# Gated linear attention with two feed-forward layers on one Trainium2 core: heads' data stored in rows 16 to 111 without gaps

## The chip, the cores and the metric

The kernel runs on one core of one Trainium2 chip. The metric is the device time of one execution in microseconds (us), lower is better. Before the change the median of 3 runs is 915.93 us (915.37 to 917.22). The profile shown here is one further execution. TensorE is called PE here, VectorE DVE, ScalarE ACT, GpSimd POOL; SP is the engine whose queue issues every DMA of this kernel.

## The reference

Three layers, one after the other. The first is a recurrence over 768 time steps for 4 batches and 8 heads of 48 dimensions; the other two are feed-forward layers of 384 to 2048 to 384 with an elementwise function between.

```python
def _attn_ref(q, k, v, alpha):                       # each (4, 8, 768, 48)
    state = np.zeros((B, H, D, D), dtype=np.float32)
    for t in range(S):
        state = alpha[:, :, t, :, None] * state + np.einsum('bhd,bhe->bhde', k[:, :, t], v[:, :, t])
        y[:, :, t] = np.einsum('bhd,bhde->bhe', q[:, :, t], state)
    return y
def _moe_ref(x, w_in, w_out, a, b):                  # x is (3072, 384), d_ff is 2048
    h = x @ w_in
    g = (a[0] + a[1]*h + a[2]*h**2 + a[3]*h**3) / (1 + abs(b[0])*abs(h) + abs(b[1])*h**2 + 1e-06)
    return g @ w_out
def _moe2_ref(x, w_in, w_out):
    h = x @ w_in
    return (h * np.cos(h)) @ w_out
```

## The kernel before

**Attention.** The sequence is cut into 6 chunks of 128 steps, and with 4 batches this makes 24 units (`NU`). A unit holds all 8 heads of one batch in one chunk: four pairs of heads (`HP`) lie side by side in the free dimension, and the two heads of a pair lie one above the other in the partitions (called rows here). A head has 48 dimensions, and its slot has 64 rows: head 0 uses rows 0 to 47, head 1 rows 64 to 111, and rows 48 to 63 and 112 to 127 hold padding (0 for keys and queries, 1 for the decay). The arrays `kqT`, `aT` and the output array `x0d` have this padding in DRAM too, so that each transfer takes 128 rows.

Per unit, `decay` makes the running product p of the decay (DVE, a scan), `guess` and `inverse0`, `inverse1` make its reciprocal (ACT, then DVE), `scale_q` and `scale_k` multiply queries by p and keys by the reciprocal (POOL, lines 310 and 305), `scores` makes the products of keys and queries (PE, L319), `mask0` and `mask1` copy and mask them (ACT, then POOL L333), `y_state` and `y_scores` make the outputs (PE, L386 and L396), `y_out` copies them from PSUM (ACT, L410) and `y_store` writes them to DRAM (L426). `transposes` (L341), `k_out` (L346), `update0` (L353) and `update1` carry the state into the next chunk.

**What sets the order.** `attention(n)` is called for slots n from -3 to 24; in slot n each stage works on its own unit: `decay` on n+3, `scale_q` and `scale_k` on n+1, `scores` on n, the outputs on n-1. The program order of each engine is the order of these calls. The loads are issued ahead, from SP, in the loop of lines 1288 to 1321:

```python
            if n >= 2:
                y_store(n - 2)
            ...
            if n >= -1:
                load(n + 5, "a")
            if n >= 0:
                load(n + 3, "kq")
                for i in range(SOME[n] if n <= LEAD else 0):
                    w_fetch(2 * NF)
                load(n + 2, "v")
```

Keys and queries (`kq`) have five buffers, the decay three, the copied outputs two (`kept[2:4]`). SP works in order, and the build gives every DMA of SP one of eight semaphores in turn; a DMA waits for the one eight places before it. Beside attention, the slots fetch the feed-forward weights (64-bit floats, `w_fetch`), which are cut into two parts by ACT, DVE and POOL (`tick`, `w_hi`, `w_lo` L212; two slots of three have one such weight tile), and from slot 8 on one `x_pieces` transfer a slot reads outputs back as the feed-forward input.

**Feed-forward layers.** From slot 20 (`LEAD`) on, `layers(n)` runs the first layer's steps, at first beside the last slots of attention, then alone; `threes(k)` runs most of the second with a scheme that needs fewer block products. These parts work on tiles of 128 rows in all dimensions, and `x_load` (lines 659 to 683) reads the attention's output array in pieces that leave out its padding rows.

**Before slot -3** the buffers' constant parts are set: `warm_up(13)` multiplies `ident` by itself, after POOL has set `ones`, the tails of `v_t`, `ident` and the tails of `s_all` (lines 1274 to 1286).

Of the kernel before, what the change touches and what calls it, by code (L numbers as in the profile page):

```python
# [24 lines left out]
NU = NC * B  # L25
H1 = 11
# [15 lines left out]
def attn_then_two_moe(ctx, tc, kqT, aT, vP, w1i, w1o, ma, mb, w2i, w2o, out):  # L42
# [5 lines left out]
    xd = [dram.tile([NC, B, 128 * HP, C], F32, name="x0d"), dram.tile([NC, DM, TB], F32, name="x1d")]  # L48
    x0d = dram.tile([2, B, 128 * HP, C], F32, name="x0")
# [64 lines left out]
    v_t = [const.tile([128, H * D + 64 - D], F32, tag=f"v{i}", name=f"v{i}") for i in range(4)]  # L114
# [3 lines left out]
    s_all = [const.tile([128, HP * D + 64 - D], F32, tag=f"s{b}", name=f"s{b}") for b in range(B)]  # L118
    s_c = [s[:, :HP * D].rearrange("p (a b) -> p a b", a=HP) for s in s_all]
# [110 lines left out]
    def load(u, name):  # L230


        if u >= NU:
            return
        c, b = divmod(u, B)
        ts = {"a": a_t, "kq": kq_t, "v": v_t}[name]
        t, src = ts[u % len(ts)], {"a": aT, "kq": kqT, "v": vP}[name][c, b]
        if name == "v":
            nc.sync.dma_start(out=t[:, :H * D], in_=src)
        elif u == 0 and name == "a":  # L240
            for cs in (slice(0, HP + HP // 2 * C), slice(HP + HP // 2 * C, HP * (C + 1))):
                nc.sync.dma_start(out=t[:, cs], in_=src[:, cs])
        else:
            nc.sync.dma_start(out=t, in_=src)
        d = U.setdefault(u, {})
        if name == "kq":
            d["k"], d["q"] = t[:, 0], t[:, 1]
        else:
            d[name] = t
# [5 lines left out]
    def sums(i, u, hs):  # L255
        at = NU if hs.start else u
        return chk[:, i, at:at + 1]


    def decay(u):  # L260
        d = U[u]
        d["p"] = in_p.tile([128, HP, C], F32, tag="p", name="p")
        a = d.pop("a")
        first, rest = a[:, :HP].unsqueeze(2), a[:, HP:].rearrange("p (a b) -> p a b", a=HP)
        for hs in parts(u):
            nc.vector.tensor_tensor(out=fresh[:, hs, 0:1], in0=first[:, hs], in1=fresh[:, hs, 1:2], op=ALU.max)
            nc.vector.tensor_tensor_scan(
                d["p"][:, hs].rearrange("p a b -> p (a b)"), rest[:, hs].rearrange("p a b -> p (a b)"),
                fresh[:, hs].rearrange("p a b -> p (a b)"), 0.0, ALU.mult, ALU.max,
            )  # L270

    def last_decay(u):
        d = U[u]
        d["pc"] = in_p.tile([128, HP, 1], F32, tag="pc", name="pc", bufs=6)
        nc.vector.tensor_tensor(out=d["pc"], in0=d["p"][:, :, C - 1:], in1=fresh[:, :, 1:2], op=ALU.max)


    def guess(u):
        d = U[u]
        d["r"] = bank("b1" if u == 1 else "r0", (128, HP, C))  # L280
# [6 lines left out]
    def inverse0(u, hs):  # L287
        d = U[u]
        if hs.start == 0:
            d["m"] = temp("ah", shape=(128, HP, C))  # L290
        nc.vector.scalar_tensor_tensor(
            d["m"][:, hs], d["p"][:, hs], RANGE, d["r"][:, hs], ALU.min, ALU.mult, accum_out=sums(1, u, hs)
        )

    def inverse1(u, hs):
        d = U[u]
        if hs.start == 0:
            d["n"] = temp("z", shape=(128, HP, C))
# [38 lines left out]
    def transposes(u):  # L337
        d = U[u]
        d["tp"] = bank("b0", (128, HP, 128))
        for hp in range(HP):  # L340
            nc.tensor.transpose(d["tp"][:, hp, :], d["k"][:, hp, :], ident)  # L341

    def k_out(u):
        d = U[u]
        d["kt"] = kept[u % 2]
        nc.scalar.activation(out=d["kt"], in_=d.pop("tp"), func=AF.Copy)  # L346

    def update0(u):
        d = U[u]
        d["u"] = ps_acc.tile([128, HP, D], F32, tag="acc2", name="u")  # L350
        for h in range(H):
            hp, j = divmod(h, 2)
            nc.tensor.matmul(  # L353
                d["u"][64 * j:64 * j + 64, hp, :], d["kt"][:, hp, 64 * j:64 * j + 64],
                d["v"][:, h * D:(h + 1) * D], start=True, stop=True,
            )

    def update1(u, tick):
        c, b = divmod(u, B)
        d = U[u]  # L360
        pc = d["pc"].to_broadcast([128, HP, D])
# [9 lines left out]
    def y_state(u):  # L371
# [48 lines left out]
    def y_store(u, rest=False):  # L420
# [5 lines left out]
        nc.sync.dma_start(out=to.rearrange("(p a) t -> p (a t)", a=HP), in_=t)  # L426
# [232 lines left out]
    def x_load(m, blk, kk):  # L659
# [7 lines left out]
        else:  # L667
            gap = (64 - D) * HP
            for p, row in {0: [(slice(0, 128), 0)], 1: [(slice(0, 64), 128), (slice(64, 128), 192 + gap)],
                           2: [(slice(0, 128), 256 + gap)]}[kk]:  # L670
                to_from = [(x, xd[0][blk])] if blk else [
                    (xt[0, 0][:, i, kk, :].bitcast(F32), x0d[i]) for i in range(2)
                ]
                for to, of in to_from:
                    rows = of[:, row:row + p.stop - p.start, :]
                    pieces.append(partial(
                        nc.sync.dma_start,
                        out=to[p].rearrange("p (b t) -> p b t", b=B), in_=rows.rearrange("b p t -> p b t")
                    ))
# [518 lines left out]
    def all_ok0():  # L1198
        nc.vector.tensor_tensor(out=chk[:, :, 0], in0=chk[:, :, 0], in1=chk[:, :, NU], op=ALU.add)
        nc.vector.tensor_scalar(ok[:, 0, :], chk[:, 0, :NU], -RANGE, None, ALU.is_ge)  # L1200
        nc.vector.tensor_scalar(ok[:, 1, :], chk[:, 1, :NU], -float(HP * C), None, ALU.add)
        nc.vector.tensor_tensor(out=ok[:, 1, :], in0=ok[:, 1, :], in1=ok[:, 1, :], op=ALU.mult)
        nc.vector.tensor_scalar(ok[:, 1, :], ok[:, 1, :], 0.0625, None, ALU.is_le)

    def all_ok1():
        cnt = bank("r1", (1, 2 * NU))
        nc.tensor.matmul(cnt, ones, ok.rearrange("p a b -> p (a b)"), start=True, stop=True)
        tot = const.tile([1, 1], F32, name="tot")
        nc.vector.tensor_reduce(tot, cnt, mybir.AxisListType.X, ALU.add)
        nc.vector.tensor_scalar(bad, tot, 128.0 * 2 * NU - 0.5, None, ALU.is_lt)  # L1210
# [52 lines left out]

    def warm_up(n):
# [5 lines left out]
    with tc.manual_schedule():  # L1270
# [13 lines left out]
        for s in s_all:  # L1284
            nc.gpsimd.memset(s[:, HP * D:], 0.0)
        warm_up(13)
        x_pieces = [p for kk in range(NK) for p in x_load(0, 0, kk)]
        for n in range(-3, NU + 1):
# [26 lines left out]
            if n == -3:  # L1315
                for name, u in (("v", 0), ("kq", 2)):
# [14 lines left out]
    def general():  # L1331
# [10 lines left out]
        for j in range(2):  # L1342
            nc.vector.memset(half[64 * j:64 * j + D, j:j + 1], 1.0)
        with tc.For_i(0, NC, 1) as c:
# [3 lines left out]
            q = fb.tile([128, B, HP, C], F32, name="q")  # L1348
            for b in range(B):
                nc.sync.dma_start(out=a[:, b], in_=aT[one, b].rearrange("o p t -> (o p) t"))  # L1350
                for i, t in enumerate((k, q)):
                    nc.sync.dma_start(out=t[:, b], in_=kqT[one, b, :, i].rearrange("o p a t -> (o p) a t"))
# [158 lines left out]
```

## Time and profile before

| | |
|---|---|
| median of 3 runs | 915.93 us (915.37 to 917.22) |
| the profiled execution's own time | 915.87 us |
| its span in the trace | 914.0 us |
| mean granted clock of PE | 0.997 of full speed |
| PE busy | 893.4 us (98% of the span) |
| DVE, ACT, POOL busy | 694.4, 697.1, 702.8 us |
| moved by DMA | 128.87 MB |

The span is the time from the first to the last recorded work; what lies around it is 1.87 us in this execution. Busy shares are means over the whole span, and the kernel has stages with different limits: attention takes about the first 105 us, and the rest is feed-forward work. So a change in attention is read in that stretch alone. A row of waits names the engine, the line that waited and what ended the wait last; a row of the chain gives start, length and what the end of the program hung on in that time.

### The profile page before, as it was taken

The page shows a single profiled execution, that of the slowest core. Times are in us where ns is not written, and L with a number is a line of the kernel's source. Part 1 is how long each engine was busy: PE and PEld are TensorE (multiplying, and loading weights), DVE is VectorE, ACT ScalarE, POOL GpSimd, SP SyncE. Part 2 cuts the span into 40 slices and gives each one's busy share as a digit, 9 for nine tenths or more (in the row PEclk, how much of TensorE's full clock was granted, in tenths as well). Part 3 has the DMA queues.
Part 4 walks back from the last instruction along what each step waited for, and adds up shares of the span by engine and source line. Part 5 has one row for each costly group of instructions (what it writes and reads, how often), then busy time and mean ns, then how long its engine had stood idle before and what let it go on. Part 6 is the DMA issues. An engine that isn't in the chain of part 4 may idle for free.

```text
span 914.0 us, 16520 instructions
## 1 busy us (share of the span) xinstructions
PE 893.4 (98%) x5732; PEld 741.5 (81%) x5732; DVE 694.4 (76%) x1247; ACT 697.1 (76%) x1302; POOL 702.8 (77%) x699
## 2 busy tenths in 40 slices
PE   8899999999999999999999999999999999999997
PEld 7788777887788888888888888878888888888885
DVE  7888889998999989979979768566367554555552
ACT  5898998989889788888788778756577666666653
POOL 7899998999889889889879668758887475655332
PEclk9999999999999999999999999999999999999999
DMA  8999743121223142233166367530243433533432
GB/s 299 336 380 379 276 131 99 57 66 40 104 82 118 44 140 59 79 95 113 43 196 187 110 219 253 196 119 27 70 139 104 157 119 90 171 104 104 139 105 90
DMA packets 67307, 128.87 MB, mean 141 GB/s; under 512 B 6928, under 2 KB 30224, under 8 KB 67216
## 3 DMA queue, kind: packets, MB, share of 16 engines
q1 hardware_dynamic: 67216, 127.74, 42.5%
q8 instruction: 47, 0.77, 0.3%
q14 instruction: 44, 0.36, 0.1%
HBM read 95.21 MB, written 32.51 MB: 140 GB/s over the span
## 4 chain that ended last, share of the span: by engine, by line
PE 73%; DVE 9%; ACT 7%; POOL 4%; DMA 4%; issue 2%; ACTq 0%; DVEq 0%; SPq 0%
PE acc L563 22%; PE b L547 18%; PE acc L1039 15%; PE b L1004 6%; PE r L1004 5%; PE r L547 4%; DMA x0d<-g 2%; DMA kq<-kqT 2%; POOL kq L305 1%; DVE g L613 1%; POOL kq L310 1%; DVE z L616 1%; ACT b L630 1%; PE b L1183 1%; DVE g L625 1%
## 5 line engine op out<-in xcount | busy, mean ns | idle before, releaser
L563 PE MATMUL acc<-hi,w 128*128 128x512 f32 x738 | 252.4, 396 | 0.0
L547 PE MATMUL b<-x,w 128*128 128x512 f32 x927 | 233.8, 397 | 1.2 <-DVE g L618 1.1
L598 POOL TENSOR_TENSOR lo<-g,hi 128x512 fp32r<-128x512 f32 x128 | 170.4, 1331 | 66.4 <-ACT hi L593 59.6
L547 PEld LDWEIGHTS b<-x,w 128*128 128x128 f32 x927 | 173.4, 188 | 45.4 <-DVE g L618 4.0
L563 PEld LDWEIGHTS acc<-hi,w 128*128 128x128 f32 x738 | 138.7, 188 | 33.9
L1096 POOL TENSOR_TENSOR lo<-g,hi 128x512 fp32r<-128x512 f32 x64 | 82.9, 1296 | 103.7 <-ACT hi L1095 91.6
L563 PE MATMUL acc<-lo,w 128*128 128x512 f32 x369 | 145.8, 395 | 0.0
L624 POOL TENSOR_TENSOR z<-z,ah 128x512 f32<-128x512 f32 x96 | 124.7, 1299 | 8.0
L1039 PE MATMUL acc<-hi,w_out 128*128 128x512 f32 x384 | 130.3, 395 | 0.0
L593 ACT ACTIVATE hi<-g 128x512 fp32r<-128x512 f32 x128 | 80.3, 628 | 47.4 <-PE acc L563 33.3
L563 PEld LDWEIGHTS acc<-lo,w 128*128 128x128 f32 x369 | 69.4, 188 | 16.5
L623 POOL TENSOR_SCALAR z<-ah,cq 128x512 f32<-128x512 f32 x96 | 74.3, 774 | 5.5 <-ACT ah L621 5.4
L1039 PE MATMUL acc<-lo,w_out 128*128 128x512 f32 x192 | 76.3, 398 | 0.4 <-POOL lo L1096 0.2
L1039 PEld LDWEIGHTS acc<-hi,w_out 128*128 128x128 f32 x384 | 68.7, 188 | 9.9
L625 DVE TENSOR_TENSOR g<-g,b 128x512 f32<-128x512 f32 x72 | 49.1, 682 | 16.2 <-ACT g L622 16.0
L621 ACT ACTIVATE ah<-b 128x512 f32<-128x512 f32 x72 | 42.7, 593 | 20.0 <-PE b L547 19.7
L547 PE MATMUL r<-x,w 128*128 128x512 f32 x225 | 56.8, 397 | 1.0 <-DVE g L618 1.0
L1081 DVE SCALAR_TENSOR_TENSOR ah<-z,b 128x512 f32<-128x512 int32 x44 | 30.2, 686 | 35.9 <-ACT z L1077 35.9
L622 ACT ACTIVATE g<-b,cq 128x512 f32<-128x512 f32 x72 | 56.0, 778 | 0.0
L618 DVE SCALAR_TENSOR_TENSOR g<-g,cq,b 128x512 f32<-128x512 f32 x72 | 53.9, 748 | 2.5
L613 DVE SCALAR_TENSOR_TENSOR g<-g,cq,b 128x512 f32<-128x512 f32 x72 | 53.5, 743 | 0.5
L630 ACT ACTIVATE b<-z,lnb 128x512 f32<-128x512 f32 x72 | 50.1, 695 | 4.7 <-DVE g L613 4.0
(201 smaller groups left out, 2030.5 us busy)
## 6 DMA issues: line engine op xcount, KB each, us to landing
w_out<-wd SPq DMA_DIRECT2D x64, 384.0 KB, 3.0
kq<-kqT SPq DMA_DIRECT2D x24, 512.0 KB, 6.5
w<-wd SPq DMA_DIRECT2D x16, 384.0 KB, 3.0
wd<-w SPq DMA_DIRECT2D x16, 384.0 KB, 2.4
a<-aT SPq DMA_DIRECT2D x23, 258.0 KB, 5.8
raw<-w2o SPq DMA_DIRECT2D x14, 384.0 KB, 3.7
v<-vP SPq DMA_DIRECT2D x24, 192.0 KB, 6.5
x<-x1d SPq DMA_DIRECT2D x18, 256.0 KB, 4.2
```

The source lines that it names most:

```text
L547: nc.tensor.matmul(h, ws[0][f][:, w, ks], x[:, xx, kk, :], start=i == 0, stop=i == 8)
L563: nc.tensor.matmul(acc[k], ws[1][f][:, w, ks], d[g], start=first and i == 0, stop=last and i == 2)
L593: nc.scalar.activation(out=t["hi"], in_=t["g"], func=AF.Copy)
L598: eng.tensor_tensor(out=t["lo"], in0=t["g"], in1=t["hi"].bitcast(F32), op=ALU.subtract)
L613: nc.vector.scalar_tensor_tensor(g, g, cq[:, 3:4], two["h"], ALU.add, ALU.mult)
L623: nc.gpsimd.tensor_scalar(zz, ah, cq[:, 1:2], cq[:, 0:1], ALU.mult, ALU.add)
L624: nc.gpsimd.tensor_tensor(out=zz, in0=zz, in1=ah, op=ALU.mult)
L625: nc.vector.tensor_tensor(out=g, in0=g, in1=h, op=ALU.mult)
L630: nc.scalar.activation(out=r, in_=two["z"], func=AF.Ln, scale=LN_S, bias=lnb)
L1004: nc.tensor.matmul(tile[:, half], w[p], x[q], start=start and i == 0, stop=True, skip_group_check=True)
L1039: nc.tensor.matmul(acc[k], item["w"][:, w, ks], item[g], start=first, stop=last)
L1096: nc.gpsimd.tensor_tensor(out=p["lo"], in0=p["g"], in1=p["hi"].bitcast(F32), op=ALU.subtract)
```

## The change

The two heads of a pair now lie in rows 16 to 63 and 64 to 111 (`GAP` is 16, `R` is 112). `kqT`, `aT` and the output arrays lose their padding: they have 96 rows instead of 128. Each load of `kq` and `a` and each `y_store` takes rows 16 to 111, 96 adjacent ones. Engines work on rows 0 to 111; rows 0 to 15 belong to head 0's slice of 64 and hold constants (0 in `kq`, 1 in `a`) that are set once per buffer before the loop. The loads of `v` are unchanged in rows and bytes. `x_load` reads the output array in three transfers a block where it were four.

```diff
+GAP = 64 - D
+R = 64 + D
+HEADS = slice(0, 64), slice(64, R)
...
-    xd = [dram.tile([NC, B, 128 * HP, C], F32, name="x0d"), dram.tile([NC, DM, TB], F32, name="x1d")]
-    x0d = dram.tile([2, B, 128 * HP, C], F32, name="x0")
+    xd = [dram.tile([NC, B, DM, C], F32, name="x0d"), dram.tile([NC, DM, TB], F32, name="x1d")]
+    x0d = dram.tile([2, B, DM, C], F32, name="x0")
...
         if name == "v":
-            nc.sync.dma_start(out=t[:, :H * D], in_=src)
+            nc.sync.dma_start(out=t[:, GAP:GAP + H * D], in_=src)
...
-            nc.sync.dma_start(out=t, in_=src)
+            nc.sync.dma_start(out=t[GAP:R], in_=src)
         d = U.setdefault(u, {})
         if name == "kq":
-            d["k"], d["q"] = t[:, 0], t[:, 1]
+            d["k"], d["q"] = t[:R, 0], t[:R, 1]
...
-                    js, ts = slice(64 * j, 64 * j + D), slice(64 * i, 64 * i + 64)
+                    js, ts = HEADS[j], slice(64 * i, 64 * i + 64)
...
-        d["tp"] = bank("b0", (128, HP, 128))
+        d["tp"] = bank("b0", (128, HP, 128))[:, :, :R]
         for hp in range(HP):
-            nc.tensor.transpose(d["tp"][:, hp, :], d["k"][:, hp, :], ident)
+            nc.tensor.transpose(d["tp"][:, hp, :], d["k"][:, hp, :], ident[:R, :R])
...
-        nc.scalar.activation(out=d["kt"], in_=d.pop("tp"), func=AF.Copy)
+        nc.scalar.activation(out=d["kt"][:, :, :R], in_=d.pop("tp"), func=AF.Copy)
...
-                d["u"][64 * j:64 * j + 64, hp, :], d["kt"][:, hp, 64 * j:64 * j + 64],
-                d["v"][:, h * D:(h + 1) * D], start=True, stop=True,
+                d["u"][HEADS[j], hp, :], d["kt"][:, hp, HEADS[j]],
+                d["v"][:, GAP + h * D:GAP + (h + 1) * D], start=True, stop=True,
...
-        nc.sync.dma_start(out=to.rearrange("(p a) t -> p (a t)", a=HP), in_=t)
+        nc.sync.dma_start(out=to.rearrange("(p a) t -> p (a t)", a=HP), in_=t[GAP:R])
...
+    def no_rest(i):
+        nc.scalar.activation(
+            out=kq_all[:GAP, i].rearrange("p a b c -> p (a b c)"),
+            in_=half_pi[:GAP].to_broadcast([GAP, 2 * HP * C]), func=AF.Copy, scale=0.0,
+        )
...
         nc.vector.memset(fresh, P_MIN)
+        nc.vector.memset(a_t[0][:GAP], 1.0)
...
         for t in v_t:
-            nc.gpsimd.memset(t[:, H * D:], 0.0)
+            nc.gpsimd.memset(t[:, :GAP], 0.0)
+            nc.gpsimd.memset(t[:, GAP + H * D:], 0.0)
...
         for s in s_all:
-            nc.gpsimd.memset(s[:, HP * D:], 0.0)
+            nc.gpsimd.memset(s[:, :GAP], 0.0)
+            nc.gpsimd.memset(s[:, GAP + HP * D:], 0.0)
+        for i in range(2):
+            nc.gpsimd.memset(kq_t[i][:GAP], 0.0)
+        nc.gpsimd.memset(a_all[:GAP, 1:], 1.0)
+        no_rest(2)
         warm_up(13)
...
             if n == -3:
+                no_rest(3)
+                no_rest(4)
                 for name, u in (("v", 0), ("kq", 2)):
```

SP, around slot 6, before (names: `x_59` is the array that the first block's outputs go to, `x0d` that of the others, `spare` a buffer for a fetched weight tile; a shape is rows x elements of a row; `DMAHW0` to `DMAHW7` are the eight semaphores of SP's DMAs):

```order
L426 DMA x0d<-g 128x512 [waits DMAHW1_49,Activation_49]
L426 DMA x_59<-x 128x512 [waits DMAHW2_49,DVE_49]
L244 DMA a<-aT 128x516 [waits DMAHW3_49,DVE_49]
L244 DMA kq<-kqT 128x1024 [waits DMAHW4_49,PE_49,Pool_49]
L163 DMA spare<-w1i 128x768 [waits DMAHW5_49]
L239 DMA v_101<-vP 128x384 [waits DMAHW6_49,PE_49]
```

and now:

```order
L430 DMA x0d<-g 96x512 [waits DMAHW1_49,Activation_49]
L430 DMA x_59<-x 96x512 [waits DMAHW2_49,DVE_49]
L247 DMA a<-aT 96x516 [waits DMAHW3_49,DVE_49]
L247 DMA kq<-kqT 96x1024 [waits DMAHW4_49,PE_49,Pool_49]
L166 DMA spare<-w1i 128x768 [waits DMAHW5_49]
L242 DMA v_101<-vP 128x384 [waits DMAHW6_49,PE_49]
```

The order and the waits are the same; four of the six transfers have 96 rows instead of 128, each row as long as before.

POOL, from the setting of `ident` to the first units of attention, before:

```order
L1280 MEMSET ident 128x128
L1281 AFFINE_SELECT ident<-ident 128x128
L1285 MEMSET s_138 128x16
L310 TENSOR_TENSOR kq<-kq,p 128x256 x2
L305 TENSOR_TENSOR kq<-kq,z 128x256 x2
```

and now:

```order
L1288 MEMSET ident 128x128
L1289 AFFINE_SELECT ident<-ident 128x128
L1293 MEMSET s_138 128x16
L1294 MEMSET s_138 128x16
L1296 MEMSET kq 16x1024 x2
L1297 MEMSET a 16x1032
L313 TENSOR_TENSOR kq<-kq,p 112x256 x2
L308 TENSOR_TENSOR kq<-kq,z 112x256 x2
```

The `s` rows stand for four buffers, one before and two now for each (and likewise for `v`, ahead of `ident`); three long memsets on 16 rows stand between them and the first `scale_q`.

## Rows read from the trace of the kernel before

**Rows 1.** Stretches: busy us of PE, PEld, DVE, ACT, POOL; PE clock; DMA share; GB/s.

```profile
20.00:105.00 85.00, 77.88 (x1550) 67.62 (x1548) 74.55 (x195) 75.78 (x153) 78.96 (x87) 1.00 1.00 365
...
250.00:914.00 664.00, 657.67 (x3257) 547.88 (x3255) 471.73 (x802) 479.99 (x889) 476.55 (x458) 1.00 0.38 120
```

**Rows 2.** Waits, 20 to 105 us (us in total, times, longest).

```profile
POOL kq L310 <- DMA kq<-kqT: 6.0, 6, 2.2
ACT g L410 <- DMA x0d<-g: 4.8, 6, 1.4
PE sc L319 <- POOL kq L305: 3.4, 10, 0.7
```

**Rows 3.** Chain, 25 to 60 us (start us, us, what).

```profile
31.14 1.09 PE b L386 x16
...
36.06 6.98 DMA x0d<-g
...
43.11 6.89 DMA kq<-kqT
...
50.07 1.28 POOL kq L310
```

**Rows 4.** Timeline of POOL, 16 to 112 us: what follows each wait for kq.

```profile
30.13 1.27 POOL L310 TENSOR_TENSOR kq<-kq,p 128x512 f32<-128x512 f32 x1 [0.96 <-DMA kq<-kqT]
...
36.07 1.27 POOL L310 TENSOR_TENSOR kq<-kq,p 128x512 f32<-128x512 f32 x1 [2.25 <-DMA kq<-kqT]
...
41.01 1.27 POOL L310 TENSOR_TENSOR kq<-kq,p 128x512 f32<-128x512 f32 x1 [0.30 <-DMA kq<-kqT]
...
50.07 1.28 POOL L310 TENSOR_TENSOR kq<-kq,p 128x512 f32<-128x512 f32 x1 [0.77 <-DMA kq<-kqT]
...
59.29 1.28 POOL L310 TENSOR_TENSOR kq<-kq,p 128x512 f32<-128x512 f32 x1
...
62.94 1.27 POOL L310 TENSOR_TENSOR kq<-kq,p 128x512 f32<-128x512 f32 x1
...
76.47 1.27 POOL L310 TENSOR_TENSOR kq<-kq,p 128x512 f32<-128x512 f32 x1 [0.64 <-DMA kq<-kqT]
...
90.41 1.27 POOL L310 TENSOR_TENSOR kq<-kq,p 128x512 f32<-128x512 f32 x1 [1.06 <-DMA kq<-kqT]
```

**Rows 5.** DMA issues, 60 to 105 us (count, KB each, median us to landing).

```profile
DMA packets 9031, 16.82 MB, mean 374 GB/s; under 512 B 866, under 2 KB 4313, under 8 KB 9021
...
kq<-kqT SPq DMA_DIRECT2D x10, 512.0 KB, 6.5
x0d<-g SPq DMA_DIRECT2D x10, 256.0 KB, 5.8
...
x<-x SPq DMA_DIRECT2D x2, 256.0 KB, 6.3
x<-x SPq DMA_DIRECT2D x3, 128.0 KB, 6.0
```

**Rows 6.** Timeline of POOL, 0 to 14 us.

```profile
1.59 0.25 POOL L1285 MEMSET s<- 128x16 f32 x4
5.74 1.41 POOL L310 TENSOR_TENSOR kq<-kq,p 128x256 f32<-128x256 f32 x2 [3.91 <-DMA kq<-kqT]
9.04 1.27 POOL L310 TENSOR_TENSOR kq<-kq,p 128x512 f32<-128x512 f32 x1 [0.53 <-DMA kq<-kqT]
12.03 1.26 POOL L305 TENSOR_TENSOR kq<-kq,z 128x512 f32<-128x512 f32 x1 [1.72 <-DVE r L266]
```

**Rows 7.** Timeline of DVE and ACT, 0 to 32 us.

```profile
3.13 0.17 DVE L266 TENSOR_TENSOR r<-a,r 128x2 f32<-128x2 f32 x1 [1.66 <-DMA a<-aT]
...
4.05 0.39 ACT L282 ACTIVATE r<-p 128x256 f32<-128x256 f32 x1 [1.96 <-DVE p L267]
...
8.93 0.60 ACT L282 ACTIVATE b<-p 128x512 f32<-128x512 f32 x1 [3.10 <-DVE p L267]
```

**Rows 8.** PE groups by form, 20 to 105 us (busy us, mean ns).

```profile
L341 PE MATMUL b<-ident,kq 128*128 128x128 f32 x72 | 11.8, 286 | 0.0
```

More of the change, by code (lines that the diff above doesn't have):

```diff
@@ L113, in attn_then_two_moe @@
     kq_t = [kq_all[:, i] for i in range(5)]
-    v_t = [const.tile([128, H * D + 64 - D], F32, tag=f"v{i}", name=f"v{i}") for i in range(4)]
+    v_t = [const.tile([128, H * D + 2 * GAP], F32, tag=f"v{i}", name=f"v{i}") for i in range(4)]
     st_all = const.tile([128, 4, DM], F32, tag="st", name="st")
     ws = [[wp.tile([128, 2, DM], F32R, tag=f"w{s}_{i}", name=f"w{s}_{i}") for i in range(NF)] for s in range(2)]
-    s_all = [const.tile([128, HP * D + 64 - D], F32, tag=f"s{b}", name=f"s{b}") for b in range(B)]
-    s_c = [s[:, :HP * D].rearrange("p (a b) -> p a b", a=HP) for s in s_all]
+    s_all = [const.tile([128, HP * D + 2 * GAP], F32, tag=f"s{b}", name=f"s{b}") for b in range(B)]
+    s_c = [s[:R, GAP:GAP + HP * D].rearrange("p (a b) -> p a b", a=HP) for s in s_all]
     w_order = sorted(
@@ L256, in sums @@
         at = NU if hs.start else u
-        return chk[:, i, at:at + 1]
+        return chk[:R, i, at:at + 1]
     def decay(u):
         d = U[u]
-        d["p"] = in_p.tile([128, HP, C], F32, tag="p", name="p")
+        d["p"] = in_p.tile([128, HP, C], F32, tag="p", name="p")[:R]
         a = d.pop("a")
@@ L273, in last_decay @@
         d = U[u]
-        d["pc"] = in_p.tile([128, HP, 1], F32, tag="pc", name="pc", bufs=6)
-        nc.vector.tensor_tensor(out=d["pc"], in0=d["p"][:, :, C - 1:], in1=fresh[:, :, 1:2], op=ALU.max)
+        d["pc"] = in_p.tile([128, HP, 1], F32, tag="pc", name="pc", bufs=6)[:R]
+        nc.vector.tensor_tensor(out=d["pc"], in0=d["p"][:, :, C - 1:], in1=fresh[:R, :, 1:2], op=ALU.max)
     def guess(u):
         d = U[u]
-        d["r"] = bank("b1" if u == 1 else "r0", (128, HP, C))
+        d["r"] = bank("b1" if u == 1 else "r0", (128, HP, C))[:R]
         for hs in parts(u):
@@ L345, in k_out @@
         d["kt"] = kept[u % 2]
-        nc.scalar.activation(out=d["kt"], in_=d.pop("tp"), func=AF.Copy)
+        nc.scalar.activation(out=d["kt"][:, :, :R], in_=d.pop("tp"), func=AF.Copy)
     def update0(u):
         d = U[u]
-        d["u"] = ps_acc.tile([128, HP, D], F32, tag="acc2", name="u")
+        d["u"] = ps_acc.tile([128, HP, D], F32, tag="acc2", name="u")[:R]
         for h in range(H):
@@ L360, in update1 @@
         d = U[u]
-        pc = d["pc"].to_broadcast([128, HP, D])
+        pc = d["pc"].to_broadcast([R, HP, D])
         if c == 0:
@@ L667, in x_load @@
         else:
[L668 to L679, printed above, removed]
+            to_from = [(x, xd[0][blk])] if blk else [
+                (xt[0, 0][:, i, kk, :].bitcast(F32), x0d[i]) for i in range(2)
+            ]
+            for to, of in to_from:
+                pieces.append(partial(
+                    nc.sync.dma_start,
+                    out=to.rearrange("p (b t) -> p b t", b=B), in_=of[:, ks, :].rearrange("b p t -> p b t")
+                ))
         if blk or m:
@@ L1198, in all_ok0 @@
     def all_ok0():
[L1199 to L1203, printed above, removed]
+        nc.vector.tensor_tensor(out=chk[:R, :, 0], in0=chk[:R, :, 0], in1=chk[:R, :, NU], op=ALU.add)
+        nc.vector.tensor_scalar(ok[:R, 0, :], chk[:R, 0, :NU], -RANGE, None, ALU.is_ge)
+        nc.vector.tensor_scalar(ok[:R, 1, :], chk[:R, 1, :NU], -float(HP * C), None, ALU.add)
+        nc.vector.tensor_tensor(out=ok[:R, 1, :], in0=ok[:R, 1, :], in1=ok[:R, 1, :], op=ALU.mult)
+        nc.vector.tensor_scalar(ok[:R, 1, :], ok[:R, 1, :], 0.0625, None, ALU.is_le)
     def all_ok1():
         cnt = bank("r1", (1, 2 * NU))
-        nc.tensor.matmul(cnt, ones, ok.rearrange("p a b -> p (a b)"), start=True, stop=True)
+        nc.tensor.matmul(cnt, ones[:R], ok[:R].rearrange("p a b -> p (a b)"), start=True, stop=True)
         tot = const.tile([1, 1], F32, name="tot")
         nc.vector.tensor_reduce(tot, cnt, mybir.AxisListType.X, ALU.add)
-        nc.vector.tensor_scalar(bad, tot, 128.0 * 2 * NU - 0.5, None, ALU.is_lt)
+        nc.vector.tensor_scalar(bad, tot, float(R) * 2 * NU - 0.5, None, ALU.is_lt)
     def layers(n):
@@ L1342, in general @@
         for j in range(2):
-            nc.vector.memset(half[64 * j:64 * j + D, j:j + 1], 1.0)
+            nc.vector.memset(half[64 * j:64 * j + 64, j:j + 1], 1.0)
         with tc.For_i(0, NC, 1) as c:
@@ L1348, in general @@
             q = fb.tile([128, B, HP, C], F32, name="q")
+            nc.vector.memset(a, 1.0)
+            nc.vector.memset(k, 0.0)
+            nc.vector.memset(q, 0.0)
             for b in range(B):
-                nc.sync.dma_start(out=a[:, b], in_=aT[one, b].rearrange("o p t -> (o p) t"))
+                nc.sync.dma_start(out=a[GAP:R, b], in_=aT[one, b].rearrange("o p t -> (o p) t"))
                 for i, t in enumerate((k, q)):
-                    nc.sync.dma_start(out=t[:, b], in_=kqT[one, b, :, i].rearrange("o p a t -> (o p) a t"))
+                    nc.sync.dma_start(out=t[GAP:R, b], in_=kqT[one, b, :, i].rearrange("o p a t -> (o p) a t"))
             a_rest = a[:, :, HP:].rearrange("p b (a t) -> p b a t", a=HP)
@@ L1490 @@
     arrays = {
-        "kqT": np.stack([slots(k, 0), slots(q, 0)], axis=3),
-        "aT": first_apart(slots(alpha, 1)),
+        "kqT": np.stack([slots(k), slots(q)], axis=3),
+        "aT": first_apart(slots(alpha)),
         "vP": vp,
```

29 lines of the change are left out of this document (14 added, 15 removed).

## The prediction

> **What bounds the kernel now.** I read the stretches first, then the waits, the chain, the timeline of POOL and the DMA issues. From 250 us on PE is busy 657.67 of 664 us [rows 1], and the change touches nothing there: that part will shift as a whole. Between 20 and 105 us, where attention runs, no engine is full: PE 77.88 of 85 us, DVE 74.55, ACT 75.78, POOL 78.96, while the DMA share is 1.00 at 365 GB/s [rows 1]. The waits name what opens the gaps: POOL waited 6.0 us for `kq` loads, in six pieces, and this is all of its idle time (85 less 78.96); ACT waited 4.8 us for stores of outputs to free their buffers; PE's longest wait is on POOL's scaled keys, 3.4 us [rows 2]. The chain says the same: until 31 us it runs on DVE and PE, then over an output store of 6.98 us to a `kq` load of 6.89 us to POOL [rows 3]. On POOL's timeline a unit with a weight tile takes 4.61 us when nothing is waited for (half of 59.29 less 50.07), one without 3.65 us (62.94 less 59.29) [rows 4].
>
> Why does a load take 6.5 us to land [rows 5]? SP has eight DMAs under way at most (the eight semaphores in the order rows). The view of this stretch lists 53 issues, and 16.82 MB over them make 0.317 MB a transfer; eight are 2.5 MB, at 374 GB/s 6.7 us. So landing time is the queue's content over its rate, and SP is held back with it.
>
> **The sum, part by part.**
>
> *Shorter transfers.* A `kq` load goes from 512 to 384 KB, an `a` load from 258 to 193.5, an output store from 256 to 192; `v` (192), weight tiles (384) and the re-reading of outputs (256 a slot from slot 8) stay. A slot with a weight tile and a re-reading moves 512 + 258 + 192 + 256 + 384 + 256 = 1858 KB now (KB of 1024 bytes), which at 374 GB/s is 5.1 us, over POOL's 4.61; without the tile 1474 KB, 4.0 us, over 3.65. After: 1601 KB, 4.4 us, and 1217 KB, 3.3 us. Both fall below POOL's times, so the queue drains between slots instead of staying full, and POOL becomes the engine that sets the pace. Then its waits go: 0.96 + 2.25 + 0.30 + 0.77 + 0.64 + 1.06 = 5.98 us [rows 4]. I do not count the first, at 30.13 us, because the chain there still runs on DVE and PE. That leaves **5.0 us**. Bounds: below nothing, if landing time does not fall; above 6.0 from POOL's row, and some 1 us more if ACT and PE, freed too, hand POOL its inputs earlier.
>
> What is late next? POOL itself. In the three slots of a pattern (two with a weight tile) it needs 4.61 + 4.61 + 3.65 = 12.87 us. PE's time per slot is not far below, so I expect it to wait for POOL a little in each slot, as in the 3.4 us of now.
>
> *POOL before the first unit.* Eight more memsets of 16 elements, at 0.25/4 = 0.06 us each [rows 6], are 0.5 us; three memsets on 16 rows of 1024, 1024 and 1032 elements are not in the trace. Lower bound 0.06 us each, as the short ones; upper bound that of POOL's two-input operation, 1.27 us for 512 elements, so 2.54 each. A memset reads no tensor, so I take half, 1.27 each and 3.8 us together. They begin at 1.84 + 0.5 = 2.3 us and end at 6.1 us. The first `scale_q` began at 5.74 after 3.91 us of waiting, so it is 0.4 us late; the next POOL operation at 9.04 waited 0.53 us, and the one at 12.03 another 1.72 us for DVE [rows 6]. The lateness is lost in those: **0**. Without this cover it would cost 0.4 us, at the upper bound 2.0 (worked out below).
>
> *DVE and ACT before the first unit.* The memset on `a` (516 elements) lies in DVE's 1.66 us before the first decay load lands; the first `no_rest` (1024 elements) lies in ACT's 1.96 us, the other two in its 3.10 us [rows 7]. An ACT pass of 512 elements takes 0.60 us, so 1024 about 1.2 by proportion, two of them 2.4: all fit, **0**. Were one not covered, it would cost its own 0.6 or 1.2 us once.
>
> *The smaller first load.* The first `a` load shrinks by a quarter, but it waits behind nothing; the chain begins with it, and I take **0**, with 0.3 us gained as the bound.
>
> *PE and ACT in a unit.* The identity in `transposes` has 112 columns instead of 128: an eighth of 11.8 us at most, 1.5 us of PE [rows 8], beside a POOL that sets the pace: **0** on the path, the bound -1.5 if PE sets it. `k_out` shrinks alike. Scores and the state's outputs sum over 64 rows for head 0 where they summed 48; as many columns stream, **0**.
>
> *Re-reading outputs.* Blocks are read in three transfers instead of four, the same bytes; 21 instead of 28 over the six blocks, and none of them stands in the waits above: **0**.
>
> Sum: -5.0 us. The profiled execution took 915.87 us (span 914.0), 0.06 below the median of 915.93, so the forecast is **910.9 us**.
>
> **A rule weighed against this.** Rows 48 to 63 and 112 to 127 were padding for every engine alike, but do the transfers really get shorter? Two kinds of re-reading stand in one stretch: pieces of 128 rows and 256 KB landed in 6.3 us, pieces of 64 rows and 128 KB in 6.0 [rows 5]. Half of the bytes gained 0.3 us; queueing explains it, but so would a limit by rows. The Trainium skill, "SBUF — State Buffer", section on the DMA port swizzle, speaks for the second: a transfer's rate follows from the ports that its rows reach, with rows 32 apart on the same port; by its table rows 16 to 111 put eight rows on half of the 16 ports, as 128 rows do, and four on the others. By that rule alone the busiest port has as much to take as before and the sum would be 0; by the bytes it is -5.0. I follow the bytes, because the queue's content over its rate gives the landing time seen, and the traffic of six kinds of transfer mixes.
>
> **The rivals.**
>
> *The transfers do not get shorter* (a limit by rows). For: the 6.0 against 6.3 us above. Against: the landing time of 6.7 us that comes out of bytes alone. The six waits stay, and the time is 915.9 us.
>
> *Another engine takes half of it.* With 85 us and POOL at 78.96, ACT 75.78 and PE 77.88 [rows 1], the others have 7 to 9 us of slack in all, and each slot hands work around all four. For: PE's waits on POOL would have to vanish for PE to follow. Against: from 50 to 76 us POOL went without a wait [rows 4], so the others can feed it. Half of 5.0 comes through: 913.4 us.
>
> *POOL's memsets delay the start* (slower). The keys of unit 1 are scaled at 12.03 us, after 1.41 + 1.41 + 1.27 = 4.09 us of POOL work since the first `scale_q` [rows 6], so the memsets may last until 7.94 us; they decide from 5.6 us together on. At the upper bound of 7.6 us they end at 9.9, the keys of unit 1 come at 14.0, 2.0 us late, and PE, DVE and ACT follow. If at the same time the loads gain nothing, the time is 917.9 us. For: no such memset is in the trace. Against: it would need 1.9 us for 1024 elements, over the 1.2 us in which ACT reads and writes as many.
>
> **How the numbers follow.** Forecast 0.56, half of it 0.20, no shorter transfers 0.16, slower 0.08. A measurement tells about 0.2% (1.8 us) from no change. The forecast and nine tenths of the half case are faster by more: 0.56 + 0.18 = 0.74; same 0.16 + 0.02 = 0.18; slower 0.08. The forecast's own range is 908.9 (7 us gained) to 912.5. For 8 in 10 it must reach to the case without gain, 916.2 with some scatter, and down to 908.0, where the start's 0.3 and part of PE's 1.5 are added to the upper bound.
>
> **What would show it.** Right: `kq` landing in 4 to 5.5 us between 20 and 105 us, a DMA share clearly below 1.00, POOL's wait for `kq` under 1 us in all, ACT's wait for stores gone, and the same feed-forward part shifted by 5 us. Half right: the loads early, but POOL waiting on ACT or DVE. Wrong: `kq` still at 6 us or more, or the first scaled keys of unit 1 after 13 us.

## Result and profile after: 3.8 us slower, with fewer bytes at a lower rate

The changed kernel takes 919.77 us (median of 8 executions, 918.68 to 926.53) beside 916.02 us (8 executions, 914.14 to 918.01) of the kernel before: a ratio of 1.0053 [1.0029, 1.0076]. The forecast was 910.9 us and the range ended at 916.2. The profiled execution took 919.06 us, its span is 917.3 us, 3.3 more than before.

The stretches of the kernel after (busy us of PE, PEld, DVE, ACT, POOL; PE clock; DMA share; GB/s):

```profile
20.00:105.00 85.00, 73.94 (x1494) 64.12 (x1490) 72.42 (x190) 71.60 (x147) 77.80 (x86) 1.00 1.04 298
250.00:917.00 667.00, 660.40 (x3269) 549.92 (x3267) 473.65 (x806) 482.61 (x894) 479.10 (x460) 1.00 0.38 121
```

The last 667 us are as the last 664 before, shifted [rows 1]. Between 20 and 105 us the DMA share stayed full while the rate fell from 365 to 298 GB/s, and every engine did less. The DMA issues from 60 to 105 us (count, KB each, median us to landing) and the waits from 20 to 105 us (us in total, times, longest):

```profile
DMA packets 7760, 13.55 MB, mean 301 GB/s; under 512 B 791, under 2 KB 4116, under 8 KB 7752
...
q1 hardware_dynamic: 7752, 13.44, 104.8%
...
kq<-kqT SPq DMA_DIRECT2D x10, 384.0 KB, 7.4
v<-vP SPq DMA_DIRECT2D x10, 192.0 KB, 7.4
x0d<-g SPq DMA_DIRECT2D x9, 192.0 KB, 6.7
```

```profile
ACT g L414 <- DMA x0d<-g: 7.3, 7, 2.5
POOL kq L313 <- DMA kq<-kqT: 7.2, 7, 1.8
PE sc L322 <- POOL kq L308: 6.5, 9, 1.3
```

A quarter fewer bytes per `kq` load, and it lands in 7.4 us where it took 6.5 [rows 5]. POOL's wait for it, which was to vanish, went from 6.0 to 7.2 us, ACT's wait for stores from 4.8 to 7.3, and PE's wait for POOL from 3.4 to 6.5 [rows 2]. The chain of after (start us, us, what) hangs on transfers for longer than before; short pieces between the rows shown are left out:

```profile
22.38 6.59 DMA kq<-kqT
...
32.97 6.42 DMA spare<-w1i
39.46 6.45 DMA x0d<-g
45.99 0.60 ACT g L414
...
48.76 6.39 DMA x0d<-g
55.22 7.75 DMA kq<-kqT
63.04 1.27 POOL kq L313
...
70.01 8.36 DMA kq<-kqT
78.44 1.28 POOL kq L313
...
96.42 8.44 DMA spare<-w1o
```

Between 20 and 105 us this chain has seven transfers, 50.4 us together; before it had five, 32.7 us together, with a store of 6.98 and a load of 6.89 us the first of them [rows 3]. The start is not to blame. POOL's timeline from 2 to 14 us:

```profile
2.10 1.83 POOL L1296 MEMSET kq<- 16x1024 f32 x2
3.89 0.95 POOL L1297 MEMSET a<- 16x1032 f32 x1
5.74 1.41 POOL L313 TENSOR_TENSOR kq<-kq,p 112x256 f32<-112x256 f32 x2 [0.91 <-DMA kq<-kqT]
...
11.82 1.26 POOL L308 TENSOR_TENSOR kq<-kq,z 112x512 f32<-112x512 f32 x1 [1.73 <-DVE r L269]
```

The new memsets take 1.83 + 0.95 = 2.78 us, the first `scale_q` begins at 5.74 us as before, and the keys of unit 1 come 0.2 us earlier than before [rows 6]. The time is lost in the middle. POOL's timeline further on:

```profile
33.55 1.27 POOL L313 TENSOR_TENSOR kq<-kq,p 112x512 f32<-112x512 f32 x1 [0.83 <-DMA kq<-kqT]
...
63.04 1.27 POOL L313 TENSOR_TENSOR kq<-kq,p 112x512 f32<-112x512 f32 x1 [1.38 <-DMA kq<-kqT]
...
107.39 1.28 POOL L313 TENSOR_TENSOR kq<-kq,p 112x512 f32<-112x512 f32 x1
```

The units that begin there began at 36.07 and 62.94 us before [rows 4], and the last of them here:

```profile
105.21 1.27 POOL L310 TENSOR_TENSOR kq<-kq,p 128x512 f32<-128x512 f32 x1
```

So the change was 2.5 us ahead early and 2.2 us behind at the end of attention: 73.84 us for what took 69.14, 6.8% more. The transfers come out close to this. Three slots with two weight tiles and re-reading move 2 x 1858 + 1474 = 5190 KB before and 2 x 1601 + 1217 = 4419 KB now; at 374 and 301 GB/s that is 14.21 and 15.03 us, 5.8% more. (Where the count starts matters: from the unit before on, which takes in the longest wait of the kernel before, it is 78.35 us for 75.08, 4.4% more. The remaining 1.1 us up to 3.3 are lost behind 107 us, where PE, after a wait of 1.60 us, ran at a granted clock of 0.50 for some 3.4 us around 119 to 122 us; the kernel before has such a stretch at 14 to 17.6 us. That this stretch costs the 1.1 us was not tried.)

What became slower, and for whom? The trace keeps each packet of a transfer, one per row. Their durations on SP's queue, 60 to 105 us, in ns, worked out from these records (mean, and median in brackets):

```
bytes of a packet       before       after        rows of the transfer, before -> after
4096 (kq)               171 (159)    239 (242)    128 -> 96
3072 (weight tiles)     126 (121)    184 (184)    128 -> 128
2064 (decay)             88 (85)      92 (85)     128 -> 96
1536 (v)                 69 (65)      88 (84)     128 -> 128
2048 (output stores)     86 (84)      95 (84)     128 -> 96
```

A row of `kq` has the same 4096 bytes as before and takes 40% longer. The rows of the weight tiles take 46% longer, though nothing of these transfers was changed: something in the new traffic slows down its neighbours. The rows of the stores and of the decay hardly change.

### The profile page after: what moved, and what is told of

Same layout as the page of the kernel before. It is cut to its first block, busy times and chain, and to the rows that moved or that the text cites. A ratio compares the mean times of both kernels' runs of the same rounds, so it can differ in the third digit from the quotient of the medians.

```text
span 917.3 us, 16519 instructions
## 1 busy us (share of the span) xinstructions
PE 891.0 (97%) x5732; PEld 739.0 (81%) x5732; DVE 694.6 (76%) x1248; ACT 698.7 (76%) x1305; POOL 705.9 (77%) x710
## 4 chain that ended last, share of the span: by engine, by line
PE 72%; DVE 8%; ACT 8%; DMA 6%; POOL 3%; issue 2%; SPq 0%; ACTq 0%; DVEq 0%
PE acc L567 22%; PE b L551 18%; PE acc L1039 15%; PE b L1004 6%; PE r L1004 5%; PE r L551 4%; DMA kq<-kqT 2%; DMA x0d<-g 1%; DVE g L617 1%; ACT b L634 1%; POOL kq L308 1%; POOL kq L313 1%; DVE z L620 1%; ACT w L205 1%; DMA spare<-w1o 1%
## 5 line engine op out<-in xcount | busy, mean ns | idle before, releaser
L215 POOL TENSOR_TENSOR w<-st,w 128x384 fp32r<-128x384 f32 x48 | 49.3, 1028 | 6.2 <-ACT w L205 6.0
```

## The experiments

Three explanations were open: a load of 96 rows is slower per byte than one of 128 (the rows decide); something else of the change costs (the arrays without gaps in DRAM, three-piece re-reading, 112-row operations); or the stores are at fault.

**Transfers alone.** Eleven stages of 24 transfers each, with nothing else running; row ranges differ, a row of SBUF always takes 4096 bytes. Two of the stages:

```diff
+        for i in range(N):
+            rows = slice(16, 112)
+            nc.sync.dma_start(out=big[i % 9][rows], in_=of(i, rows))
+        drain()
...
+        for i in range(N):
+            rows = (slice(0, 128), slice(16, 112))[i % 2]
+            nc.sync.dma_start(out=big[i % 9][rows], in_=of(i, rows))
+        drain()
```

> No attention and no feed-forward work: stages of 24 transfers of 4096 bytes a row between DRAM and nine buffers, one stage after the other, loads first: rows 0-127; 16-111; 0-95; 0-95 and 32-127 in turn; 0-63; 0-63 and 64-127 in turn; 0-127 and 16-111 in turn; 0-47 and 64-111 in turn; 16-47, 48-79 and 80-111 in turn; then stores of rows 0-127 and of 16-111. The output is zeros. Theory A (rows decide: a transfer waits for the fullest group of rows that share a way into SBUF, so 96 adjacent rows cost what 128 cost): per transfer about 1.3 us for 0-127, 16-111, 0-95 and 0-63 alike; evened out over two transfers 0-95 with 32-127 falls to about 1.0 and 0-63 with 64-127 to about 0.7. Theory B (a transfer of other than 128 rows is split so that DMA engines get into each other's way, even or not): 0-95 with 32-127 in turn is as slow as 16-111 alone, 1.3 us or more. Theory C (bytes decide, and the loss comes from elsewhere in the change): 16-111 and 0-95 take 0.98 us, three quarters of 0-127. Stores: A and B allow either; C says 0.75.

One execution was profiled. The stretches inside the stages, each with the queue full of that stage's transfers (busy us of DVE and POOL; PE clock; DMA share; GB/s), in this order: loads to rows 0 to 127; 16 to 111; 0 to 95; 0 to 95 and 32 to 127 in turn; 0 to 63; 0 to 63 and 64 to 127 in turn; 0 to 127 and 16 to 111 in turn; then, after two stages left out here, stores of 128 rows and of rows 16 to 111.

```profile
18.00:34.00 16.00, 0.58 (x1) 0.00 (x0) 1.00 1.03 411
44.00:62.00 18.00, 0.45 (x1) 0.00 (x0) 1.00 1.03 279
78.00:100.00 22.00, 0.80 (x1) 0.00 (x0) 1.00 1.03 277
113.00:135.00 22.00, 0.27 (x1) 0.00 (x0) 1.00 1.03 278
147.00:168.00 21.00, 1.41 (x2) 0.00 (x0) 1.00 1.03 211
177.00:194.00 17.00, 0.91 (x1) 0.00 (x0) 1.00 1.03 237
208.00:232.00 24.00, 0.00 (x0) 0.00 (x0) 1.00 1.03 278
...
284.00:304.00 20.00, 2.05 (x3) 0.00 (x0) 1.00 1.02 405
316.00:336.00 20.00, 0.00 (x0) 0.00 (x0) 1.00 0.95 300
```

Time per transfer is its bytes over the rate. A load of 128 rows takes 524,288 bytes / 411 GB/s = 1.28 us, one of rows 16 to 111 takes 393,216 / 279 = 1.41 us: a quarter of the bytes gone, and it takes a tenth longer. (From 8 to 28 us, with the filling of the queue counted in, the first stage has 385 GB/s; the next experiment with transfers alone was planned with that figure.) Moving the 96 rows about from transfer to transfer does not even it out (278 GB/s), so theory A's relief does not come, and theory C's 0.98 us does not come either. The two kinds in turn, which is nearest to what the changed kernel sends, run at 278 GB/s too, the rate of the 96-row loads alone: 458,752 / 278 = 1.65 us on average, where half of 1.28 and 1.41 would be 1.34. So the mixture as a whole loses the rate that the 128-row loads have alone. That is the sign of the result: the loads of 96 rows gain nothing for themselves, and the loads beside them lose. The stores behave alike when alone, 1.29 us for 128 rows and 1.31 for 96. The two stages left out, 48 rows and 32 rows a transfer, had DMA shares of 0.78 and 0.61, so they were bound by something else and say nothing here.

**Loads of 128 rows, stores of 96.** The rest of the change stays; `kqT` and `aT` get their padding rows back, as constants above and below the 96, so the memsets fall away.

```diff
-            nc.sync.dma_start(out=t[GAP:R], in_=src)
+            nc.sync.dma_start(out=t, in_=src)
...
-        for i in range(2):
-            nc.gpsimd.memset(kq_t[i][:GAP], 0.0)
-        nc.gpsimd.memset(a_all[:GAP, 1:], 1.0)
-        no_rest(2)
```

> The changed kernel with its loads of keys, queries and decay taken over 128 rows again (arrays padded above and below rows 16-111, and the constants of the outer rows come with the loads, so the memsets before the loop fall away); the outputs' stores keep 96 rows. Theories A and B (the 96-row loads slow the DMA engines): 4096-byte packets take 160 ns again as before the change, POOL's wait for kq falls below 6 us, 912 to 916.5 us. Theory C (something else in the change): stays at 919 to 921.

913.78 us (12 executions, 912.81 to 914.47), ratio to the kernel before 0.9978 [0.9965, 0.999]. The change without its smaller loads is faster than the kernel before. Its stretch:

```profile
20.00:105.00 85.00, 78.43 (x1572) 68.49 (x1568) 75.53 (x197) 78.42 (x158) 82.38 (x91) 1.00 0.99 357
```

POOL is up from 77.80 to 82.38 us. The packets of weight tiles are back at 129 ns on average, those of `kq` at 171 (60 to 105 us).

**Loads of 96 rows, stores of 128**, and **both of 128.** Here the output array has its padding rows (the second kernel joins this edit with the one above):

```diff
-    xd = [dram.tile([NC, B, DM, C], F32, name="x0d"), dram.tile([NC, DM, TB], F32, name="x1d")]
+    y_all = [dram.tile([NC, B, 128 * HP, C], F32, name="x0d"), dram.tile([2, B, 128 * HP, C], F32, name="x0")]
+    xd = [y_all[0][:, :, GAP * HP:R * HP, :], dram.tile([NC, DM, TB], F32, name="x1d")]
...
-        nc.sync.dma_start(out=to.rearrange("(p a) t -> p (a t)", a=HP), in_=t[GAP:R])
+        nc.sync.dma_start(out=to.rearrange("(p a) t -> p (a t)", a=HP), in_=t)
```

> The changed kernel with the outputs' stores over 128 rows again (output array padded); the loads keep 96 rows. Theories A and B: the loads are the cause, so it stays slow, and the larger stores add bytes: 919 to 922 us. If the 96-row stores are the cause instead: 913 to 916.

> The changed kernel with loads and stores over 128 rows: what is left of the change is the heads in rows 16-63 and 64-111 and engines that work on 112 rows. Theories A and B: 915 to 917 us, as before the change. Theory C: 919 to 921.

Stores of 128 with loads of 96: 920.97 us (7 executions, 919.76 to 928.27), ratio 1.007 [1.0041, 1.0099]. Both of 128: 914.73 us (12, 912.81 to 916.35), ratio 0.9988 [0.9975, 1.0001]. The second says that all the rest of the change (rows 16 to 111, 112-row operations, re-reading in three) is worth 0.9 us or nothing. (It lies just below the 915 to 917 us expected.) The stores are not at fault: in the company of 128-row loads, 96-row stores are 914.73 - 913.78 = 0.95 us better in the medians, which is at the edge of the noise, and with 96-row loads they are not worse.

**One load at a time, and loads with stores.** Transfers alone again. Twelve loads into one buffer, so that each waits for the last, of 128 rows and then of rows 16 to 111; then, with the queue full, rows 0 to 111; rows 0 to 63 and 64 to 95 in turn; then loads and stores in turn. One execution was profiled.

```diff
+        for i in range(N // 2):
+            rows = slice(16, 112)
+            nc.sync.dma_start(out=big[0][rows], in_=of(i, rows))
...
+            rows, part = slice(16, 112), slice(0, 128)
+            nc.sync.dma_start(out=big[i % 9][rows], in_=of(i, rows))
+            nc.sync.dma_start(out=scratch[i % 9][part], in_=more[part])
```

> No attention and no feed-forward work, transfers of 4096 bytes a row alone, in stages: loads of rows 0-127 each waiting for the one before; the same of rows 16-111; loads of rows 0-111; of rows 0-63 and 64-95 in turn; then a load and a store in turn: both of 128 rows, load of 128 with store of 96, load of 96 with store of 128. The output is zeros. Theory B1 (the engines of one 96-row transfer already get into each other's way): a single 96-row load takes no less time than a single 128-row load, both near 3 us, and packets of 4096 bytes spread above 160 ns in it. Theory B2 (only several transfers in the queue do): the single 96-row load is 0.2 to 0.3 us shorter and its packets keep 160 ns. Rows 0-111: both say slower than 128 rows by rate (below 330 GB/s, against 385). In the mixed stages: if only loads into SBUF suffer, the pair with the 96-row store keeps the rate of the pair of 128 or loses under 10 per cent, and the pair with the 96-row load falls by over 15 per cent; if stores suffer as much, both fall.

DMA issues, 20 to 40 us, loads of 128 rows one by one (count, KB each, median us to landing), then the same of 60 to 90 us, whose first row is the last 96-row loads of that kind:

```profile
big<-src SPq DMA_DIRECT2D x7, 512.0 KB, 3.3
```

```profile
big<-src SPq DMA_DIRECT2D x8, 384.0 KB, 3.2
```

Alone in the queue, the 96-row load lands 0.1 us earlier, so three quarters of the bytes buy 3% at most. That lies between theory B1 (nothing) and B2 (0.2 to 0.3 us). The stretches of the other stages (columns as above), in this order: rows 0 to 111; 0 to 63 and 64 to 95 in turn; load and store of 128; load of 128 with store of 96; load of 96 with store of 128:

```profile
92.00:120.00 28.00, 3.31 (x4) 0.00 (x0) 1.00 1.03 277
124.00:146.00 22.00, 6.38 (x7) 0.00 (x0) 1.00 0.97 239
160.00:200.00 40.00, 1.46 (x2) 0.00 (x0) 1.00 1.03 420
214.00:260.00 46.00, 3.65 (x4) 0.00 (x0) 1.00 1.03 420
266.00:305.00 39.00, 0.39 (x1) 0.00 (x0) 1.00 1.03 407
```

Rows 0 to 111 were expected below 330 GB/s and are: 458,752 bytes / 277 GB/s = 1.66 us, so a load of 112 rows takes 30% longer than one of 128. Loads of 112 and of 96 rows have the same rate. The mixture with stores was a miss. I expected the rate of the pair with a 96-row load to fall by over 15%; it is 407 GB/s beside 420, 3% lower. So with a store beside every load the loss hardly shows. In the kernel the stores are 192 of a slot's 1601 KB, and there the loss does show. Why stores take the loss away was not tried further.

**Which load it is.** In one kernel only the decay loads have 96 rows, in the other only those of keys and queries:

```diff
-            nc.sync.dma_start(out=t[GAP:R], in_=src)
+            nc.sync.dma_start(out=t if name == "kq" else t[GAP:R], in_=src)
```

```diff
-            nc.sync.dma_start(out=t[GAP:R], in_=src)
+            nc.sync.dma_start(out=t[GAP:R] if name == "kq" else t, in_=src)
```

> The changed kernel with keys and queries loaded over 128 rows (padded array, their memsets fall away), decay loads and output stores of 96 rows. Theory B (every load of other than 128 rows slows all loads that are under way beside it): between the kernel with all loads of 128 (913.8) and the changed one (919.8), nearer to the first: 914.5 to 917.5; the 3072-byte packets of the weight tiles, never changed themselves, rise from 121 ns to 130 to 165 on average. If only the large kq loads matter: 913 to 914.5, and the weights' packets stay at 121 to 123.

> The changed kernel with the decay loaded over 128 rows (padded array, its memset falls away), keys, queries and stores of 96 rows. Theory B: most of the loss stays: 916.5 to 920.5, weights' packets at 150 to 190 ns. If decay loads are the cause: 913 to 915.

Only the decay: 916.87 us (10 executions, 914.43 to 919.8), ratio 1.0013 [0.9995, 1.0031]. Only keys and queries: 922.62 us (6, 920.68 to 926.11), ratio 1.0066 [1.0042, 1.009], above the range expected. Against 0.9978 with neither, the decay's 96 rows cost 0.35% or 3.2 us, those of `kq` 0.88% or 8.1 us, and both together (1.0053, 1.0049) no more than `kq` alone. The costs do not add. The stretch of the kernel with only `kq` at 96:

```profile
20.00:105.00 85.00, 70.38 (x1438) 61.41 (x1437) 69.50 (x182) 69.36 (x142) 75.99 (x83) 0.99 1.05 302
```

Its queue is as full as that of the change and nearly as slow (302 and 298 GB/s), with 64.5 KB more of decay in each slot. So once `kq` has slowed the queue, taking rows from the decay as well only takes bytes away. That fits the numbers but was not tested by itself. The packets of weight tiles grow with each step: 129 ns with no load at 96, 136 beside the decay's 96 rows (337 GB/s from 20 to 105 us), 185 beside those of `kq`.

**The same bytes in 128 rows.** If only the way from bytes to time was wrong in the prediction, then the bytes of the change, taken from columns instead of rows, should give the forecast. The kernel with loads of 128 rows is cut to 768 of 1024 columns of `kq` and 387 of 516 of the decay, so it leaves out part of the work's input:

```diff
+KQ, AC = 2 * HP * C * 3 // 4, HP * (C + 1) * 3 // 4
...
-            nc.sync.dma_start(out=t, in_=src)
+            flat = t[:, :AC] if name == "a" else t.rearrange("p a b c -> p (a b c)")[:, :KQ]
+            nc.sync.dma_start(out=flat, in_=src)
```

> The kernel with loads of 128 rows and stores of 96 (e2), but each load of keys and queries takes 768 of its 1024 columns and each load of decay 387 of 516: as many bytes as the change moves, in 128 rows. It leaves out the second half of each unit's queries and the last quarter of its decay, whose columns stay at constants set once. If the prediction's sum was right and only its step from rows to transfer time was wrong: kq lands in 4 to 5.5 us, POOL's wait for kq falls under 1 us, DMA share below 0.95, 910 to 912.5 us. If bytes were never worth anything here (POOL sets the pace already in e2): 913 to 914.5.

911.73 us (9 executions, 911.22 to 912.87), ratio 0.9951 [0.9934, 0.9968], or 4.4 us less than the kernel before (916.12 beside it). Its stretch from 20 to 105 us, its waits there and its DMA issues from 60 to 105 us:

```profile
20.00:105.00 85.00, 79.74 (x1621) 69.90 (x1618) 76.94 (x202) 79.42 (x161) 83.89 (x93) 1.00 0.93 317
```

```profile
POOL kq L315 <- DMA kq<-kqT: 1.0, 2, 0.8
ACT g L416 <- DMA x0d<-g: 0.5, 1, 0.5
```

```profile
DMA packets 7940, 13.58 MB, mean 302 GB/s; under 512 B 791, under 2 KB 4628, under 8 KB 7930
...
kq<-kqT SPq DMA_DIRECT2D x9, 384.0 KB, 5.1
x0d<-g SPq DMA_DIRECT2D x9, 192.0 KB, 3.5
```

The same 384 KB land in 5.1 us instead of 7.4, the DMA share falls to 0.93, POOL waits 1.0 us for `kq`, and POOL at 83.89 of 85 us sets the pace. From 60 to 105 us both kernels move as much, 13.58 and 13.55 MB; here the queue has room to spare, there it is full.

**The change and its better version side by side.** The change as it is, and the kernel with 128-row loads and 96-row stores, once more on one chip, beside the kernel before.

> The changed kernel once more, on the same chip and beside the same runs of before as e8 and e10, so that their distances don't rest on two chips: 918.5 to 921.

> The kernel of e2 once more, as the candidate that beats both, beside the change: 913 to 914.5 us, 0.1 to 0.3 per cent under before and 5 to 7 us under the change.

The change: 920.72 us (12 executions, 918.53 to 926.64), ratio 1.0049 [1.0032, 1.0067]. With 128-row loads: 913.17 us (12, 911.92 to 915.35), ratio 0.9969 [0.9955, 0.9983]. The second is faster than both kernels, by 0.3% than the one before and by 7.55 us than the change, a little more than the 5 to 7 expected, with no execution of the one in the range of the other. The change also scatters more. Its profiled execution took 926.64 us this time; there POOL waited twice as long for `kq` as in the profile above, and the packets of `kq` took 266 ns on average. Its stretch from 20 to 105 us and a row of its waits there:

```profile
20.00:105.00 85.00, 69.03 (x1388) 58.21 (x1383) 65.02 (x172) 64.70 (x134) 71.06 (x78) 1.00 1.02 277
```

```profile
POOL kq L313 <- DMA kq<-kqT: 13.9, 11, 3.0
```

## Why the prediction was wrong

**What bounds attention: right.** A full queue and POOL's waits for `kq` set the pace before. The kernel with fewer columns shows it: with landing at 5.1 us, POOL's and ACT's waits are all but gone, and 4.4 us with them.

**Shorter transfers, the term of -5.0 us: wrong, and this is the step that failed.** "Landing time is the queue's content over its rate" held: the view of after lists 47 transfers with 13.44 MB from 60 to 105 us, eight of them are 2.29 MB, and at 301 GB/s these take 7.6 us; 7.4 were measured. (The view of before lists 52 issues where I wrote 53; with 52 my 6.7 us become 6.9, and nothing hangs on it.) What failed is the rate. I put 374 GB/s under the smaller slots ("I follow the bytes"), as if the rate belonged to the queue. It depends on the rows of the loads: 411 GB/s for 128, 279 for 96, and 278 where the two alternate. With the rate of after, a slot with a tile and re-reading takes 1601 KB / 301 GB/s = 5.4 us, longer than the 5.1 of before, where I had 4.4 and a queue that drains. `kq` landing at 7.4 us is what the prediction itself had named as a sign of being wrong. The comparison with columns isolates this step: the same bytes in 128 rows gave -4.4 us and POOL's wait for `kq` fell from 6.0 to 1.0 us, so POOL's times and the condition "below 4.61 and 3.65 us" were sound.

The size of the sum was in part lucky. I left out the wait of 0.96 us because the chain still ran on the engines beside it, but I counted the 2.25 us that ended at 36.07 us, where the same holds. The chain of before reaches the store only there:

```profile
34.33 0.60 ACT g L346
...
35.68 0.38 ACT b L72
36.06 6.98 DMA x0d<-g
```

By that rule the sum was 5.98 - 0.96 - 2.25 = 2.8 us. The 4.4 us measured are nearer to the 5.0, but no run shows what each wait was worth.

**The rule that I weighed and put aside.** Loads of rows 16 to 111 took 1.41 us where loads of 128 took 1.28. By the Trainium skill, "SBUF — State Buffer", section on the DMA port swizzle, an estimate is that with eight rows on the fullest port as before the time stays and the rate is three quarters, 308 GB/s from the measured 411. The 279 measured are a tenth below that, so the trace agrees with the direction and with most of the size. For rows 0 to 111 the Trainium skill's table in the same section has eight rows on the fullest port again and the time would stay at 1.28 us; 1.66 us were measured, so there the trace does not agree. The Trainium skill, "SBUF — State Buffer", section on two DMAs that are to hit both halves, also says that the ports are picked by the rows of a single transfer and that two transfers can't be fused; the 278 GB/s of loads to rows 0 to 95 and 32 to 127 in turn, against 277 for rows 0 to 95 alone, agree. My reason against the rule, traffic of six kinds that mixes, was turned round by the runs: the mixture goes at the rate of its slower kind. By the rule alone the sum was 0; the result is +3.8 us.

**The evidence in the rows of before.** The pieces of 128 rows landed in 6.3 us and those of 64 rows in 6.0 [rows 5]. I let queueing explain this. Queued as they were, these landing times cannot tell a limit by bytes from one by rows: a transfer lands after what is queued ahead of it, whatever its own size. Nothing in the kernel before showed many loads of fewer rows in a row, so the price had to be bounded, and below nothing too. My lower bound was "nothing gained", without a reason that excludes a loss.

**The rivals.** "The transfers do not get shorter" named the cause and priced it at 915.9 us, with a chance of 0.16: it was nearly right on the loads alone (1.41 us for 1.28) and left out what they do to others. "Another engine takes half" did not arise. "POOL's memsets delay the start", the only slower case, did not happen: the three long ones took 2.78 us where I estimated 3.8, and ended 0.91 us before the first `kq` load was there.

**The terms at nothing: right as far as seen.** The kernel with loads and stores of 128 rows keeps rows 16 to 111, the 112-row operations and the re-reading in three, and measures 0.9988 [0.9975, 1.0001], not told from no change. The smaller first load let DVE's first decay begin 0.2 us earlier (2.94 us, before at 3.13), inside the bound of 0.3. PE's transposes fell from 13.3 to 12.1 us over their 80 matmuls of the first 125 us, against a bound of 1.5 and beside PE's longer waits for POOL. The keys of unit 1 were scaled at 11.82 us, before the 13 that I named as the sign of delay.

**What was late next: right where it could be seen.** POOL sets the pace once the queue drains: with fewer columns it is busy 83.89 of 85 us at a DMA share of 0.93. With 128-row loads it is busy 82.38 us, and the queue is still full (0.99).

**Left open.** The packets' records don't say which of the 16 DMA engines or which way into SBUF a packet took. So it is shown that 96-row loads take no less time than 128-row ones and slow these down; by what means is not. That loads of 112 and 96 rows and mixtures all came out at 277 to 279 GB/s fits theory B, that any load of other than 128 rows sets the DMA engines against each other, better than theory A, a count of rows on the fullest way in. Loads of 64 rows are the exception (211 GB/s).

## What to carry to other kernels

Padding rows in a load can be free: before taking them out, measure loads of that very row range, alone and in turn with the other loads of the queue, and read the rate, not the bytes. Where bytes have to go, take them from the columns of 128-row loads first; rows taken from stores did no harm here. And when the neighbours' packets of unchanged size get longer in a trace, look for the cause in the traffic before you look at the engines that wait.

## What was not expected of the hardware

- A mixture of these loads goes at the rate of its slower kind: 278 GB/s for 128 and 96 rows in turn, against 411 (128 rows) and 279 (96 rows) alone; in the kernel, unchanged packets of 3072 bytes went from 126 to 184 ns.
- A load of rows 0 to 111 takes longer than one of all 128: 1.66 us against 1.28.
- Loads of 64 rows were nearly as slow as of 128: 262,144 bytes at 211 GB/s are 1.24 us a transfer, and moving them between the halves gave 237 GB/s, 12% more.
- Stores of 96 rows alone also take as long as those of 128 (1.31 and 1.29 us), yet in the kernel no harm of theirs shows. With a store beside every load, the loss of the 96-row load was 3% (407 GB/s beside 420).
